# A fused attention and expert kernel whose attention order is planned anew

## The chip, the cores and the metric

The kernel runs on one core of a Trainium2 chip. The metric is the device time of one execution in microseconds (us). TensorE (PE) multiplies matrices and writes to PSUM, VectorE (DVE), ScalarE (ACT) and GpSimd (POOL) work on tiles, and SyncE's queue (SP) issues the transfers. PEld is TensorE's load of stationary operands, which overlaps its matmuls.

## What is computed

Causal attention over 2 x 12 heads of 448 positions and 64 channels, then two expert layers on the 896 x 768 result, all in fp32:

```python
scores = scale * np.matmul(q, k.transpose(0, 1, 3, 2))
scores = np.where(mask, -1000000000.0, scores)          # causal
attn = np.exp(scores - np.max(scores, axis=-1, keepdims=True))
attn = attn / (np.sum(attn, axis=-1, keepdims=True) + 1e-09)
x = np.matmul(attn, v)          # then heads side by side: 896 x 768
h = np.maximum(np.maximum(x @ w1, x @ w2), x @ w3)      # 768 -> 768
y = h @ w_out
u = y @ w_in                                            # 768 -> 2048
g = np.where(u > 0.0, u, np.exp(np.minimum(u, 0.0)) - 1.0)
out = g @ w_out2
```

The weights arrive as 64-bit words (the host's view of doubles) and are made into two fp32r parts, hi and lo, on the chip.

## The kernel before

Heads go in 12 pairs (`pair(p)`). The keys and queries of a head are cut into blocks of 128: three full ones and a last one of 64 (`R`). For a pair, in order of what needs what:

- `load` brings q and k of both heads (448 KB), `load_v` brings v (256 KB, keys padded with zeros to 512), both on SP's queue. Three buffers each.
- `scores` in three groups (`SCORES`, g = 0 for query blocks 2 and 0, g = 1 for the last block, g = 2 for block 1) into PSUM banks named `s`; there are 4 (`SBANKS`), and a pair needs 5: two heads times groups 0 and 2, and one bank for both heads' group 1.
- `least` (VectorE, L268) adds the mask, negates, stores the tile `pr` and reduces each row; it frees the score bank. `exps` (ScalarE, L278) takes the exponential and sums it into `l`.
- `guard` (GpSimd, L282) adds 1e-9 to the sums, `inverse` (VectorE, L287) takes the reciprocal, `normalise` (GpSimd, L291) multiplies the rows, seven tiles a pair.
- `turn` (five groups, `TURNS`, 16 transposes of 128 columns a pair) transposes blocks into PSUM banks named `pt`, of which there are two; `turned` (ScalarE or VectorE, L207) copies them to `th`, and the last block's 64 keys to `th_r`.
- `values` (L325) multiplies with v, four steps a pair: three over 128 keys and a last one (c = 3) over the 64 last keys. fp32 products stand as two instructions each in the trace.
- `x_hi` (ScalarE) and `x_lo` (VectorE) split the result for the expert layers.

Three blocks of the first expert layer (`AHEAD`, tile `ph`, 18 matmuls each) and the making of their weights (`weight_steps`, L142 to L159) are put among the attention's work.

The order is not written by hand. Every step is a task of the class `Plan`, with a cost per engine that it may run on, tasks that it follows, buffers that it takes and gives, and a rank. `order` repeats: for each task whose predecessors are placed it works out when it could begin and on which engine it would end first; it takes the earliest beginning; among the tasks of that engine that could begin within `SLACK` of it, it places the one of least rank. `LAG` is the planned time from an engine's end to another's start, `SWITCH` what a change of matmul kind (`mode`) adds to TensorE's start. What comes out is issued in that order, so each engine's queue and SP's queue run it as it stands. Before, rank is (pair, number of the step), `SWITCH` is 90 ns and `SLACK` 100 ns.

Behind the attention the products of the expert layers follow in program order; the conversion of their first weight (f = 1) is issued after the last `x_lo`.

Of the kernel before, what the change touches and what calls it, by code (L numbers as in the profile page):

```python
# [8 lines left out]
F32 = mybir.dt.float32  # L9
# [19 lines left out]
W_LEAST = 2.0 ** -15  # L29
W_MOST = 122876.0  # L30
AHEADS = 3
PAIRS = 3
THS = 2
SBANKS = 4


class Plan:
# [6 lines left out]


    LAG = {"PE": 210, "ACT": 150, "DVE": 125, "POOL": 90, "DMA": 2000}
    SLACK = 100
    SWITCH = 90

    def __init__(self, slots):  # L50
        self.slots = {k: [0] * n for k, n in slots.items()}
        self.parts, self.tasks, self.mode = {}, [], None

    def add(self, fn, args, engines, rank, after=(), takes=(), gives=(), mode=None):
        t = {"fn": fn, "args": args, "engines": engines, "rank": rank, "after": [a for a in after if a],
             "takes": list(takes), "gives": list(gives), "mode": mode}
        self.tasks.append(t)
        return t

    def begins(self, t, free):  # L60
        ready = {}
        for e, cost in t["engines"].items():
            at = free[e] + (self.SWITCH if e == "PE" and t["mode"] != self.mode else 0)
            for a in t["after"]:
                at = max(at, a["end"] + (0 if a["eng"] == e else self.LAG[a["eng"]]))
            for k in set(t["takes"]):
                n = t["takes"].count(k)
                if len(self.slots[k]) < n:
# [35 lines left out]
def fused_kernel(ctx: ExitStack, tc: tile.TileContext, qk, v, w1, w2, w3, wo, wi2, wo2, outT):  # L104
    nc = tc.nc
# [75 lines left out]
    with ExitStack() as s1:  # L181
# [13 lines left out]
        with ExitStack() as s2:  # L195
# [15 lines left out]
            def warm(eng, n):  # L211

                idle = ps_m.tile([128, 512], F32, tag="m", name="idle")
                for _ in range(n):
                    nc.tensor.matmul(idle, ones, ones_row, start=True, stop=True)

            plan.add(warm, (8,), {"PE": 3500}, (-1,), takes=["m"], gives=["m"])

# [3 lines left out]

            TURNS = (((0, 0, (0, 1, 2)),), ((1, 0, (0, 1, 2)),), ((0, 1, (1, 2)), (1, 1, (1, 2))),
                     ((0, 2, (2,)), (1, 2, (2,)), (None, NB, (NB,))), tuple((None, c, (NB,)) for c in range(NB)))

            def heads(i):
                return (None,) if i == NB else (1, 0)

            def pair(p):
# [97 lines left out]

# [7 lines left out]

                if p == 0:
                    cut = (slice(0, 2 * C), slice(2 * C, S))
                    got = [plan.add(load, (part,), {"DMA": 1000}, (p, 0), takes=["qk"] * (n == 0))  # L340
                           for n, part in enumerate(cut)]
                    order = (2, 0, 1)
                else:
                    got = [plan.add(load, (slice(0, S),), {"DMA": 2000}, (p, 0), takes=["qk"])]
                    order = (0, 1, 2)
                got_v = plan.add(load_v, (), {"DMA": 1000}, (p, 0.5), takes=["v"])
                done, first = {}, None
                for g in order:
                    need = got[:1] if g == 2 else got
                    ws = [min(C * (i + 1), S) for i in SCORES[g]]  # L350
                    js = heads(SCORES[g][0])
                    s = plan.add(
                        scores, (g,), {"PE": sum(120 + int(1.67 * w) for w in ws)}, (p, 1), need, takes=["s"] * len(js),
                        gives=["qk"] * (g == order[-1]), mode="s")
                    for j in js:
                        a = plan.add(
                            least, (g, j), {"DVE": sum(75 + int(1.06 * w) for w in ws)}, (p, 2), [s, first],
                            takes=["pr"] * (first is None), gives=["s"])
                        first = first or a
                        a = plan.add(exps, (g, j), {"ACT": sum(278 + int(0.84 * w) for w in ws)}, (p, 3), [a])  # L360
                        for i in SCORES[g]:
                            done[i, j] = a
                flat = {}
                for part in PARTS:
                    mine = [ij for ij, n in COLS.items() if part[0] <= n < part[1]]
                    a = plan.add(guard, part, {"POOL": 240}, (p, 4), [done[ij] for ij in mine])
                    a = plan.add(inverse, part, {"DVE": 65}, (p, 4), [a])
                    for i, j in sorted(mine, key=lambda ij: -ij[0]):
                        w = min(C * (i + 1), S)
                        flat[i, j] = plan.add(normalise, (i, j), {"POOL": 240 + int(0.84 * w)}, (p, 5), [a])  # L370
                ths, begun = [], None
                for t, blocks in enumerate(TURNS):
                    need = {(i, j) for j, c, q in blocks for i in q}
                    n = sum(len(q) for _, _, q in blocks)
                    a = plan.add(
                        turn, (t,), {"PE": 108 * n}, (p, 6), [begun] + [flat[ij] for ij in sorted(need, key=str)],
                        takes=["pt"] + ["th"] * (t == 0), gives=[("pr", p, len(TURNS))], mode="pt")
                    begun = begun or a
                    ths.append(plan.add(
                        turned, (t,), {"ACT": 55 + int(0.84 * C * n) + 60 * (t == 3),  # L380
                                       "DVE": 70 + int(1.04 * C * n) + 70 * (t == 3)},
                        (p, 7), [a], gives=["pt"]))
# [6 lines left out]
                a = plan.add(x_hi, (), {"ACT": 420}, (p, 9), [prev])  # L389
                return plan.add(x_lo, (), {"DVE": 540}, (p, 9), [a], gives=["m"])  # L390

            xs_done = [pair(p) for p in range(B * NPAIR)]

# [2 lines left out]
            def weights(k):  # L396
# [8 lines left out]
                for s, (eng, cost) in enumerate((  # L405
                        ("DMA", 4200), ("DVE", 580), ("DVE", 580), ("DVE", 580), ("DVE", 920), ("DVE", 920),
                        ("ACT", 740), ("DVE", 830))):
                    t = plan.add(
                        step, (), {eng: cost}, (GATES[k] + 1.9, s), [t or xs_done[GATES[k]]], takes={0: ["raw"], 1: ["f"]}.get(s, []),
                        gives={5: ["raw"], 7: ["f"]}.get(s, []))  # L410
                return t

            def block(k, ready):
# [14 lines left out]

                t = ready
                for c in range(NK):  # L430
                    t = plan.add(product, (c,), {"PE": 610}, (20 + k if c == 0 else 0, c), [t, ready, xs_done[c if k == 0 else NK - 1]],
                        takes=["m"] * (c == 0), mode="x")
                return plan.add(keep, (), {"DVE" if n else "ACT": 540 if n else 420}, (0, k), [t], gives=["m"])

            kept = None
            for k in range(len(AHEAD)):
# [123 lines left out]
```

## Time and profile before

| | us |
|---|---|
| median of three runs | 508.65 (508.29 to 509.17) |
| the profiled execution, its own time | 505.65 |
| its span, first to last instruction | 503.9 |
| TensorE busy in the span | 496.9 |
| VectorE, ScalarE, GpSimd busy | 364.5, 186.5, 51.9 |

In the rows below a timeline row is: start, duration, engine, line, operation, written tile <- read tiles, tile of the array (rows x columns, for TensorE), shape, count, and in brackets the idle time before it with what ended it. Consecutive instructions of one kind are merged in one row. TensorE's matmuls are pipelined and their ends are modelled, so starts are read, not ends.

### The profile page before, as it was taken

How to read it: one execution, taken by the hardware profiler on the slowest of the kernel's cores; microseconds unless marked ns; L12 is line 12 of the kernel's file. 1: busy time of each engine (PE TensorE's matmuls, PEld its weight loads, DVE VectorE, ACT ScalarE, POOL GpSimd, SP SyncE). 2: the span in 40 equal slices, each digit the busy share in tenths (PEclk: the TensorE clock that was granted, in tenths of full speed). 3: DMA queues.
4: the chain of work that ended last, by engine and by line, in shares of the span. 5: the costliest groups of instructions: out<-in, count | busy, mean ns of one | idle time of the engine just before them, and what ended most of it. 6: DMA issues, size and time to landing. Idle time of an engine off the chain costs nothing.

```text
span 503.9 us, 6971 instructions
## 1 busy us (share of the span) xinstructions
PE 496.9 (99%) x2600; PEld 426.2 (85%) x2600; DVE 364.5 (72%) x687; ACT 186.5 (37%) x432; POOL 51.9 (10%) x119
## 2 busy tenths in 40 slices
PE   8999999999999999999999999999999999999997
PEld 3556755699999999999999999999999999999996
DVE  4687966289987877787787898889878667667310
ACT  5978778422222122122214445545544111111100
POOL 3856365200000000000000000000000000000000
PEclk9999999999999999999999999999999999999999
DMA  6435720023532333233223323313332344344000
GB/s 212 154 117 170 246 84 24 1 110 141 185 129 69 120 125 123 75 117 126 88 100 126 87 101 125 123 68 124 104 88 80 118 149 144 112 152 140 1 36 36
DMA packets 13968, 55.88 MB, mean 111 GB/s; under 512 B 1520, under 2 KB 3568, under 8 KB 13936
## 3 DMA queue, kind: packets, MB, share of 16 engines
q1 hardware_dynamic: 13936, 55.45, 33.3%
q8 instruction: 20, 0.33, 0.3%
q14 instruction: 12, 0.10, 0.1%
HBM read 52.69 MB, written 2.75 MB: 110 GB/s over the span
## 4 chain that ended last, share of the span: by engine, by line
PE 93%; DVE 2%; ACT 2%; DMA 1%; POOL 1%; issue 1%; SPq 0%; POOLq 0%; ACTq 0%; DVEq 0%
PE ph L173 9%; PE ph L174 9%; PE ph L176 9%; PE pg L173 8%; PE pg L174 8%; PE pg L176 8%; PE po L176 8%; PE po L174 8%; PE po L173 8%; PE s L254 4%; PE pt L301 4%; PE o L325 3%; PE py L173 3%; PE py L176 3%; PE py L174 3%; DMA qk<-in_qk 1%
## 5 line engine op out<-in xcount | busy, mean ns | idle before, releaser
L173 PE MATMUL ph<-x,hi_w 128*128 128x448 f32 x216 | 79.3, 367 | 0.0
L174 PE MATMUL ph<-x,hi_w 128*128 128x448 f32 x216 | 78.9, 365 | 0.0
L173 PE MATMUL pg<-y,hi_wi 128*128 128x448 f32 x192 | 70.6, 367 | 0.0
L174 PE MATMUL pg<-y,hi_wi 128*128 128x448 f32 x192 | 70.6, 367 | 0.0
L173 PE MATMUL po<-g,hi_wo 128*128 128x448 f32 x192 | 70.1, 365 | 0.0
L174 PE MATMUL po<-g,hi_wo 128*128 128x448 f32 x192 | 70.1, 365 | 0.0
L159 ACT CAST hi_wo<-f_wo 128x768 fp32r<-128x768 f32 (+1 forms) x24 | 18.8, 783 | 125.3 <-PE po L174 56.4
L176 PE MATMUL ph<-x,lo_w 128*128 128x448 f32 x216 | 64.2, 365 | 0.0
L176 PE MATMUL po<-g,lo_wo 128*128 128x448 f32 x192 | 55.3, 365 | 0.0
L176 PE MATMUL pg<-y,lo_wi 128*128 128x448 f32 x192 | 55.0, 367 | 0.0
L126 DVE TENSOR_TENSOR lo_wo<-f_wo,hi_wo 128x768 fp32r<-128x768 f32 (+1 forms) x24 | 21.4, 891 | 32.1 <-ACT hi_wo L159 32.1
L173 PEld LDWEIGHTS ph<-x,hi_w 128*128 128x128 f32 x216 | 40.6, 188 | 3.3
L176 PEld LDWEIGHTS ph<-x,lo_w 128*128 128x128 f32 x216 | 40.6, 188 | 3.2
L174 PEld LDWEIGHTS ph<-x,hi_w 128*128 128x128 f32 x216 | 40.6, 188 | 3.1
L159 ACT CAST hi_w<-f_w 128x768 fp32r<-128x768 f32 x18 | 15.1, 837 | 73.3 <-PE ph L174 45.4
L173 PEld LDWEIGHTS pg<-y,hi_wi 128*128 128x128 f32 x192 | 36.0, 188 | 3.4
L176 PEld LDWEIGHTS pg<-y,lo_wi 128*128 128x128 f32 x192 | 36.0, 188 | 3.4
L174 PEld LDWEIGHTS pg<-y,hi_wi 128*128 128x128 f32 x192 | 36.0, 188 | 3.4
L174 PEld LDWEIGHTS po<-g,hi_wo 128*128 128x128 f32 x192 | 36.1, 188 | 2.9
L176 PEld LDWEIGHTS po<-g,lo_wo 128*128 128x128 f32 x192 | 36.1, 188 | 2.9
L173 PEld LDWEIGHTS po<-g,hi_wo 128*128 128x128 f32 x192 | 36.0, 188 | 2.8
L278 ACT ACTIVATE pr<-pr,nmx 128x384 f32<-128x384 f32 (+1 forms) x72 | 35.8, 502 | 5.4 <-DVE nmx L268 5.0
(76 smaller groups left out, 814.7 us busy)
## 6 DMA issues: line engine op xcount, KB each, us to landing
raw_w<-in_w SPq DMA_DIRECT2D x18, 768.0 KB, 4.4
raw_wi<-in_wi SPq DMA_DIRECT2D x16, 768.0 KB, 4.3
raw_wo<-in_wo SPq DMA_DIRECT2D x12, 768.0 KB, 4.4
raw_wo<-in_wo SPq DMA_DIRECT2D x12, 640.0 KB, 4.0
qk<-in_qk SPq DMA_DIRECT2D x11, 448.0 KB, 3.4
v<-in_v SPq DMA_DIRECT2D x12, 256.0 KB, 2.7
out_t<-ot SPq DMA_DIRECT2D x12, 224.0 KB, 3.2
qk<-in_qk SPq DMA_DIRECT2D x1, 256.0 KB, 3.3
```

The costliest lines, as they stand in the source:

```text
L126: return eng.tensor_tensor(out=out, in0=a, in1=b.bitcast(F32), op=ALU.subtract)
L159: nc.scalar.copy(hi, fb)
L173: nc.tensor.matmul(ps, hi[:, c, :], xs[cc][:, 0, :], start=(cc == 0), stop=False)
L174: nc.tensor.matmul(ps, hi[:, c, :], xs[cc][:, 1, :], start=False, stop=False)
L176: nc.tensor.matmul(ps, lo[:, c, :], xs[cc][:, 0, :], start=False, stop=(cc == total - 1))
L254: nc.tensor.matmul(out, u["qk"][own, 0, C * i:w], u["qk"][own, 1, :w], start=True, stop=True, skip_group_check=True)
L278: nc.scalar.activation(pr, pr, AF.Exp, bias=u["nmx"][:, n:n + 1], scale=-1.0, accum_out=u["l"][:, n:n + 1])
L301: nc.tensor.transpose(pt[:e - C * c, at:at + C], u["pr", j, i][:, C * c:e], ident)
L325: nc.tensor.matmul(u["o"][D * j:D * (j + 1), C * c:], u["v"][:R, j, c] if c == NB else u["v"][:, j, c], u["th_r"][:, j] if c == NB else u[ ...
```

## The change

Ranks are now pair + lead, with one lead per kind of work (table `LEADS`), ties in order of addition. `SLACK` is 80. A change of matmul kind has a charge by the two kinds. Four pairs may hold their tiles in place of three, and a pair takes its place at its first scores instead of its first `least`. `guard` and `normalise` may run on VectorE or GpSimd, whichever would end first in the plan. The last keys' tile `th_r` has 128 rows; two such tiles are set to zero once by GpSimd, only the first 64 rows are written later, and the product reads all 128 rows of both operands. Some planned costs are altered (loads, scores, values, warming), which changes the plan and no instruction.

```diff
-PAIRS = 3
+PAIRS = 4
+LEADS = {
+    "exps": 12.19, "guard": 2.16, "inverse": 4.13, "keep": -4.94, "least": 4, "load": -9.21, "load_v": -4.69,
+    "normalise": 5.1, "product": 17.18, "scores0": -0.81, "scores1": 1.15, "scores2": 0.27, "step": -5.89,
+    "turn0": -10.05, "turn1": 0.24, "turn2": 1.83, "turn3": 1.96, "turn4": 1.17, "turned0": -7.64, "turned1": 8.07,
+    "turned2": 12.56, "turned3": -1.06, "turned4": 10.91, "values0": 2.99, "values1": 2.02, "values2": -11.03,
+    "values3": -0.06, "warm": -14.64, "x_hi": 3, "x_lo": -5.37,
+}
-    SLACK = 100
-    SWITCH = 90
+    SLACK = 80
+    SWITCH = {("s", "pt"): 150, ("pt", "s"): 95, ("pt", "x"): 0, ("x", "pt"): 0, ("o", "pt"): 60}
+    SWITCHES = 100
...
+    def switch(self, mode):
+        return 0 if mode == self.mode else self.SWITCH.get((self.mode, mode), self.SWITCHES)
...
-            at = free[e] + (self.SWITCH if e == "PE" and t["mode"] != self.mode else 0)
+            at = free[e] + (self.switch(t["mode"]) if e == "PE" else 0)
...
-            plan.add(warm, (8,), {"PE": 3500}, (-1,), takes=["m"], gives=["m"])
+            plan.add(warm, (8,), {"PE": 4200}, 0, takes=["m"], gives=["m"])
...
+            th_r = [thp.tile([C, 2, R], F32, name=f"th_r{n}", bufs=1) for n in range(THS)]
+            for t in th_r:
+                nc.gpsimd.memset(t, 0.0)
...
-                        u["th_r"] = thp.tile([R, 2, R], F32, tag="th_r", name=f"th_r{p}")
+                        u["th_r"] = th_r[p % THS]
...
-                            copy(eng, u["th_r"], pt[:R, 2 * w:2 * w + C].rearrange("k (j q) -> k j q", j=2))
+                            copy(eng, u["th_r"][:R], pt[:R, 2 * w:2 * w + C].rearrange("k (j q) -> k j q", j=2))
...
-                            u["o"][D * j:D * (j + 1), C * c:], u["v"][:R, j, c] if c == NB else u["v"][:, j, c],
+                            u["o"][D * j:D * (j + 1), C * c:], u["v"][:, j, c],
...
-                        scores, (g,), {"PE": sum(120 + int(1.67 * w) for w in ws)}, (p, 1), need, takes=["s"] * len(js),
-                        gives=["qk"] * (g == order[-1]), mode="s")
+                        scores, (g,), {"PE": (960, 870, 540)[g]}, p, [*need, begun],
+                        takes=["s"] * len(js) + ["pr"] * (begun is None), gives=["qk"] * (g == order[-1]), mode="s")
...
-                    a = plan.add(guard, part, {"POOL": 240}, (p, 4), [done[ij] for ij in mine])
+                    a = plan.add(guard, part, {"POOL": 240, "DVE": 65}, p, [done[ij] for ij in mine])
...
-                        flat[i, j] = plan.add(normalise, (i, j), {"POOL": 240 + int(0.84 * w)}, (p, 5), [a])
+                        flat[i, j] = plan.add(
+                            normalise, (i, j), {"POOL": 240 + int(0.84 * w), "DVE": 60 + int(0.62 * w)}, p, [a])
...
-                        values, (c,), {"PE": 120 + int(1.67 * (S - C * c))}, (p, 8),
-                        [ths[t] for t in need] + [got_v, prev], takes=["m"] * (c == 0),
-                        gives=["th", "v"] * (c == NB), mode="o" if c < NB else "r")
+                        values, (c,), {"PE": (805, 540, 380, 130)[c]}, p, [ths[t] for t in need] + [got_v, prev],
+                        takes=["m"] * (c == 0), gives=["th", "v"] * (c == NB), mode="o")
```

The expert blocks' first products rank at k + 17.18 and their other products at -20 + 17.18; the weights' steps at the pair of their gate - 5.89. The other ranks follow the table.

## Rows read from the trace of the kernel before

**Rows 1.** The page, busy us, share of the span, instructions.

```profile
PE 496.9 (99%) x2600; PEld 426.2 (85%) x2600; DVE 364.5 (72%) x687; ACT 186.5 (37%) x432; POOL 51.9 (10%) x119
```

**Rows 2.** Stretches: length, busy us by engine, granted clock, DMA share, GB/s.

```profile
0.00:100.97 100.97, 97.51 (x638) 57.90 (x638) 64.35 (x240) 75.41 (x239) 51.88 (x119) 1.00 0.39 126
100.97:500.50 399.53, 399.42 (x1966) 368.32 (x1962) 300.15 (x447) 110.58 (x193) 0.00 (x0) 1.00 0.32 107
```

**Rows 3.** TensorE's timeline, the first scores.

```profile
4.26 3.12 PE L254 MATMUL s<-qk 64*128 64x256 f32 x16
8.44 4.84 PE L254 MATMUL s<-qk 64*128 64x384 f32 x28 [1.06 <-DMA qk<-in_qk]
```

**Rows 4.** SP's issues near 2 us; their transfers, us to landing last.

```profile
2.07 0.59 SPq L242 DMA_DIRECT2D v<-in_v  x1
...
2.70 0.43 SPq L238 DMA_DIRECT2D qk<-in_qk  x1
...
v<-in_v SPq DMA_DIRECT2D x1, 256.0 KB, 5.1
...
qk<-in_qk SPq DMA_DIRECT2D x1, 448.0 KB, 5.6
```

**Rows 5.** TensorE's timeline, one period in the middle of the attention.

```profile
64.68 1.84 PE L325 MATMUL o<-th,v 128*64 128x448 f32 x12
66.45 0.33 PE L325 MATMUL o<-th_r,v 64*64 64x64 f32 x4
66.71 0.87 PE L301 MATMUL pt<-ident,pr 128*128 128x128 f32 x6
67.51 0.70 PE L254 MATMUL s<-qk 64*128 64x256 f32 x4
68.14 0.88 PE L301 MATMUL pt<-ident,pr 128*128 128x128 f32 x6
68.86 0.27 PE L301 MATMUL pt<-ident,pr_None 128*64 128x128 f32 x1
69.06 1.14 PE L254 MATMUL s<-qk 64*128 64x384 f32 x8
70.13 0.55 PE L301 MATMUL pt<-ident,pr_None 128*128 128x128 f32 x3
70.60 0.97 PE L254 MATMUL s<-qk 64*64 64x448 f32 x4
71.50 1.84 PE L325 MATMUL o<-th,v 128*64 128x448 f32 x12
```

**Rows 6.** The same timeline, two groups of scores in a row.

```profile
56.72 1.57 PE L254 MATMUL s<-qk 64*128 64x256 f32 x12
58.21 0.47 PE L173 MATMUL ph<-x,hi_w 128*128 128x448 f32 x1
```

**Rows 7.** Stretches again: the next period, columns as in rows 2.

```profile
71.50:78.32 6.82, 6.82 (x50) 3.81 (x48) 4.27 (x22) 5.89 (x20) 3.85 (x10) 1.00 0.16 41
```

**Rows 8.** The same timeline, first and last of four waits within the attention.

```profile
35.78 0.44 PE L301 MATMUL pt<-ident,pr 128*128 128x128 f32 x2 [0.25 <-ACT th L207]
...
98.94 1.84 PE L325 MATMUL o<-th,v 128*64 128x448 f32 x12 [0.57 <-ACT th L207]
```

**Rows 9.** GpSimd's and VectorE's timelines: four normalisings, weight steps, together and apart.

```profile
28.82 3.28 POOL L291 TENSOR_SCALAR pr<-pr,r 128x384 f32<-128x384 f32 x4 [0.38 <-DVE r L287]
...
73.92 1.85 POOL L291 TENSOR_SCALAR pr<-pr,r 128x384 f32<-128x384 f32 x4 [0.38 <-DVE r L287]
...
29.14 0.83 DVE L144 TENSOR_SCALAR f_w<-f_w 128x768 f32<-128x768 f32 x1
...
113.34 0.56 DVE L144 TENSOR_SCALAR f_w<-f_w 128x768 f32<-128x768 f32 x1
```

**Rows 10.** Timelines of VectorE and TensorE where the next weight is first read.

```profile
109.55 1.81 DVE L126 TENSOR_TENSOR lo_w<-f_w,hi_w 128x768 fp32r<-128x768 f32 x2
...
112.01 0.36 PE L173 MATMUL ph<-x,hi_w 128*128 128x448 f32 x1
```

More of the change, by code (lines that the diff above doesn't have):

```diff
@@ L52, in __init__, with add @@
         self.parts, self.tasks, self.mode = {}, [], None
-    def add(self, fn, args, engines, rank, after=(), takes=(), gives=(), mode=None):
-        t = {"fn": fn, "args": args, "engines": engines, "rank": rank, "after": [a for a in after if a],
-             "takes": list(takes), "gives": list(gives), "mode": mode}
+    def add(self, fn, args, engines, pair, after=(), takes=(), gives=(), mode=None):
+        lead = LEADS.get(f"{fn.__name__}{args[0]}" if args else None, LEADS.get(fn.__name__))
+        t = {"fn": fn, "args": args, "engines": engines, "pair": pair, "rank": (pair + lead, len(self.tasks)),
+             "after": [a for a in after if a], "takes": list(takes), "gives": list(gives), "mode": mode}
         self.tasks.append(t)
         return t
+    def switch(self, mode):
+        return 0 if mode == self.mode else self.SWITCH.get((self.mode, mode), self.SWITCHES)
     def begins(self, t, free):
@@ L339, in pair @@
                     cut = (slice(0, 2 * C), slice(2 * C, S))
-                    got = [plan.add(load, (part,), {"DMA": 1000}, (p, 0), takes=["qk"] * (n == 0))
+                    got = [plan.add(load, (part,), {"DMA": 1000 if n else 2200}, p, takes=["qk"] * (n == 0))
                            for n, part in enumerate(cut)]
@@ L343, in pair @@
                 else:
-                    got = [plan.add(load, (slice(0, S),), {"DMA": 2000}, (p, 0), takes=["qk"])]
+                    got = [plan.add(load, (slice(0, S),), {"DMA": 2000}, p, takes=["qk"])]
                     order = (0, 1, 2)
-                got_v = plan.add(load_v, (), {"DMA": 1000}, (p, 0.5), takes=["v"])
-                done, first = {}, None
+                got_v = plan.add(load_v, (), {"DMA": 1200}, p, takes=["v"])
+                done, begun = {}, None
                 for g in order:
@@ L352, in pair @@
                     s = plan.add(
-                        scores, (g,), {"PE": sum(120 + int(1.67 * w) for w in ws)}, (p, 1), need, takes=["s"] * len(js),
-                        gives=["qk"] * (g == order[-1]), mode="s")
+                        scores, (g,), {"PE": (960, 870, 540)[g]}, p, [*need, begun],
+                        takes=["s"] * len(js) + ["pr"] * (begun is None), gives=["qk"] * (g == order[-1]), mode="s")
+                    begun = begun or s
                     for j in js:
[L356 to L360, printed above, removed]
+                        a = plan.add(least, (g, j), {"DVE": sum(75 + int(1.06 * w) for w in ws)}, p, [s], gives=["s"])
+                        a = plan.add(exps, (g, j), {"ACT": sum(278 + int(0.84 * w) for w in ws)}, p, [a])
                         for i in SCORES[g]:
@@ L365, in pair @@
                     mine = [ij for ij, n in COLS.items() if part[0] <= n < part[1]]
-                    a = plan.add(guard, part, {"POOL": 240}, (p, 4), [done[ij] for ij in mine])
-                    a = plan.add(inverse, part, {"DVE": 65}, (p, 4), [a])
+                    a = plan.add(guard, part, {"POOL": 240, "DVE": 65}, p, [done[ij] for ij in mine])
+                    a = plan.add(inverse, part, {"DVE": 65}, p, [a])
                     for i, j in sorted(mine, key=lambda ij: -ij[0]):
                         w = min(C * (i + 1), S)
-                        flat[i, j] = plan.add(normalise, (i, j), {"POOL": 240 + int(0.84 * w)}, (p, 5), [a])
+                        flat[i, j] = plan.add(
+                            normalise, (i, j), {"POOL": 240 + int(0.84 * w), "DVE": 60 + int(0.62 * w)}, p, [a])
                 ths, begun = [], None
@@ L375, in pair @@
                     a = plan.add(
-                        turn, (t,), {"PE": 108 * n}, (p, 6), [begun] + [flat[ij] for ij in sorted(need, key=str)],
+                        turn, (t,), {"PE": 109 * n}, p, [begun] + [flat[ij] for ij in sorted(need, key=str)],
                         takes=["pt"] + ["th"] * (t == 0), gives=[("pr", p, len(TURNS))], mode="pt")
@@ L380, in pair @@
                         turned, (t,), {"ACT": 55 + int(0.84 * C * n) + 60 * (t == 3),
-                                       "DVE": 70 + int(1.04 * C * n) + 70 * (t == 3)},
-                        (p, 7), [a], gives=["pt"]))
+                                       "DVE": 70 + int(1.04 * C * n) + 70 * (t == 3)}, p, [a], gives=["pt"]))
                 prev = None
@@ L385, in pair @@
                     prev = plan.add(
-                        values, (c,), {"PE": 120 + int(1.67 * (S - C * c))}, (p, 8),
-                        [ths[t] for t in need] + [got_v, prev], takes=["m"] * (c == 0),
-                        gives=["th", "v"] * (c == NB), mode="o" if c < NB else "r")
-                a = plan.add(x_hi, (), {"ACT": 420}, (p, 9), [prev])
-                return plan.add(x_lo, (), {"DVE": 540}, (p, 9), [a], gives=["m"])
+                        values, (c,), {"PE": (805, 540, 380, 130)[c]}, p, [ths[t] for t in need] + [got_v, prev],
+                        takes=["m"] * (c == 0), gives=["th", "v"] * (c == NB), mode="o")
+                a = plan.add(x_hi, (), {"ACT": 420}, p, [prev])
+                return plan.add(x_lo, (), {"DVE": 540}, p, [a], gives=["m"])
             xs_done = [pair(p) for p in range(B * NPAIR)]
@@ L408, in weights @@
                     t = plan.add(
-                        step, (), {eng: cost}, (GATES[k] + 1.9, s), [t or xs_done[GATES[k]]], takes={0: ["raw"], 1: ["f"]}.get(s, []),
+                        step, (), {eng: cost}, GATES[k], [t or xs_done[GATES[k]]], takes={0: ["raw"], 1: ["f"]}.get(s, []),
                         gives={5: ["raw"], 7: ["f"]}.get(s, []))
@@ L430, in block @@
                 for c in range(NK):
-                    t = plan.add(product, (c,), {"PE": 610}, (20 + k if c == 0 else 0, c), [t, ready, xs_done[c if k == 0 else NK - 1]],
+                    t = plan.add(product, (c,), {"PE": 610}, k if c == 0 else -20, [t, ready, xs_done[c if k == 0 else NK - 1]],
                         takes=["m"] * (c == 0), mode="x")
-                return plan.add(keep, (), {"DVE" if n else "ACT": 540 if n else 420}, (0, k), [t], gives=["m"])
+                return plan.add(keep, (), {"DVE" if n else "ACT": 540 if n else 420}, 0, [t], gives=["m"])
             kept = None
```

## The prediction

> **What bounds the kernel now.** I read the page's busy shares first: TensorE is busy 99% of the span [rows 1], so only time on TensorE's queue counts. The stretches come next. Up to 100.97 us stand the attention and three early expert blocks; from there to 500.50 us TensorE is busy 399.42 of 399.53 us [rows 2], at the full granted clock (1.00, the 2.4 GHz level). The change leaves all work behind the attention as it is, so it can move the time only by ending the attention earlier, and whatever is won there passes to the end one for one, as long as the first weight tile of the next part still comes in time (below). TensorE's order of time then shows what those 100.97 us are made of. The first scores start at 4.26 us and the next ones wait 1.06 us for a load [rows 3]. From there TensorE is nearly without a gap: four waits, 1.27 us in all, of which the first and the longest stand in [rows 8]. One pair's period in the middle of the stage is 6.82 us (64.68 to 71.50) and holds no wait at all [rows 5], while ScalarE is busy 5.89 us of it, VectorE 4.27 and GpSimd 3.85 [rows 7]. So the stage is bound by TensorE, and what is left in a period is what TensorE pays when it goes from one kind of matmul to another.
>
> That price can be read from the starts in [rows 5]. Six, seven and three transposes take 0.80, 0.92 and 0.47 us to the next kind: 0.11 us each and 0.14 us for the visit. Scores of 256, 512 and 448 columns take 0.63, 1.07 and 0.90 us; two such groups in a row (768 columns) take 58.21 - 56.72 = 1.49 us [rows 6] against 0.63 + 1.07 = 1.70 apart, so a visit to the scores costs 0.21 us. A period has three visits to the transposes, three to the scores, one to the values. The last-keys products (four instructions, 64x64) take 66.71 - 66.45 = 0.26 us.
>
> **The change, part by part.** The sum is made against the profiled execution (505.65 us, span 503.9); the median of the three runs without a profile is 508.65, 3.0 us longer, and I carry the difference over to it.
>
> (a) First loads. Ranks of equal start decide among loads, and the new leads put every load of q and k (-9.21) ahead of every load of v (-4.69). So the first seven issues on SP become q/k of pair 0 (two), q/k of pairs 1 and 2, then the three of v. Now v of pair 0 goes ahead of pair 1's q and k: issued at 2.07 and 2.70 us, landed 5.1 and 5.6 us later, at 7.2 and 8.3 [rows 4]. The 448 KB between those landings took 1.1 us, so taking 256 KB out of the way brings pair 1's load forward by 256/448 x 1.1 = 0.6 us, 0.7 with the earlier issue. The wait is 1.06 us, the gain lies between 0.6 and 1.06; I take 0.7, the lower row, because the bytes ahead set it. The v that is moved back then lands at some 7.6 + 1.1 + 0.6 = 9.3 us by the same rate; TensorE is at scores until 13.2 us [rows 3], so nobody reads it before. The new charge of 4200 for the warming matmuls alters planned times alone; they are the same eight matmuls.
>
> (b) Last keys over zero rows. The four 64x64 instructions become 128x64 ones, as the twelve before them are. By columns at the rate of those twelve (1.77 us for 448 + 320 + 192 = 960 columns [rows 5], 1.84 ns a column) 64 columns are 0.12 us against 0.26. No row shows a 128x64 fp32 product of 64 columns, so it is bounded: 0 saved if 0.26 is a floor for four short instructions, 0.14 if columns rule. I take 0.13, near the upper end, because a transpose, also short, runs at 0.11 a piece with nothing added inside its visit. Twelve pairs: 1.6 us (0 to 1.7). The two added memsets of 128 columns fall on GpSimd's queue before its first guard, where it idles for microseconds; the copy into the 64 used rows is unchanged.
>
> The row says only that four small matmuls cost as much as 140 columns. The Trainium skill, "TensorEngine Tiling", section Key Properties, says that a change of tiling mode, unlike a change of tile, drains TensorE; by it the 0.26 holds a drain from 128x64 to 64x64 that (b) removes. The same page's section Instruction Overhead puts some 60 cycles on every matmul however short, by which part of the 0.26 would stay. By the first the sum is as I give it, by the second alone it is up to 1.6 us less.
>
> (c) Fewer changes of kind. Before, a change costs 90 ns in the plan and SLACK is 100, so a change of kind never put a task out of reach and rank alone chose. After, a change to or from the scores is charged 95 to 150 and SLACK is 80: a task of the kind that TensorE is in wins wherever one is ready. How far this goes is bounded by banks: two hold transposes, so after two turns the third waits for a copy, and five turns a pair make at least 2.5 visits in place of 3. Four hold scores, of which a pair needs five: 1.25 visits at least. At the least, nothing is saved; at the most (3 - 2.5) x 0.14 + (3 - 1.25) x 0.21 = 0.44 us a pair, 4.8 us over eleven periods. ScalarE's 5.89 us a period, still 0.9 us below TensorE's, does not stop this. I take 0.18 a pair, half a visit of each kind (0.07 + 0.105), 2.0 us: the leads also rank kinds, and a bank that is freed too late breaks a run of one kind.
>
> (d) Four pairs held, and normalising on VectorE too. They give the plan more ready work where TensorE waits: the four gaps (1.27 us [rows 8]). The two longest lie at the end, where only the last pair is left and nothing but an expert block could fill them. I take 0.4 us (0 to 1.27).
>
> (e) What VectorE's new work costs. It gets some of the seven normalisings and guards a pair, against them GpSimd is lightened. On its own a 768-wide tensor_scalar takes it 0.56 us, so a 384-wide one about 0.3 by halves (an estimate). But the trace shows the two engines hindering one another: four normalisings that take GpSimd 1.85 us take 3.28 when VectorE runs two tensor_scalars beside them, and those take 0.83 instead of 0.56 [rows 9]. Behind such an instruction on VectorE are queued the reductions that free score banks, and TensorE waits for those; GpSimd's late tiles hold the next transposes. The plan has no term for this. Nothing lost at the least, since both engines have over 2.5 us of idle time a period; at the most each pair loses 0.6 us (below). I take 0.6 us in all.
>
> Sum: 0.7 + 1.6 + 2.0 + 0.4 - 0.6 = 4.1 us less, 501.5 for the profiled execution, **504.5 us** for the median.
>
> Cover behind the attention: the conversion of the next weight starts at the last pair's x, its two low parts end at 111.36 us, and TensorE reads the first at 112.01 [rows 10]: 0.65 us of slack at least. It moves with the attention's end, so I cost it at nothing; if the last x came over 0.65 us later after the last values than now, the rest would be a TensorE gap.
>
> **The rivals.**
> First, the collision of VectorE and GpSimd sets the pace (slower). Its place is each pair's normalising; its price is what [rows 9] show, 3.28 - 1.85 = 1.43 us on GpSimd for four tiles, of which TensorE sees what goes beyond the turn's slack. It outweighs the gain from 4.7/11 = 0.43 us of TensorE wait a pair; at 0.55 a pair the time is 508.65 - 4.7 + 6.1 = 510.0. For it: a static order with thinner slack, and a plan without this term. Against: after today's collision at 29 to 32 us TensorE's first wait is 0.25 us, at 35.78 [rows 8], and it names a copy.
>
> The Trainium skill, "SBUF — State Buffer", section Who interferes with whom, states that GpSimd and a VectorE tensor_scalar in a two-port mode exclude each other for a whole instruction. The trace agrees in that both were lengthened, and by that rule this rival is the mechanism to fear.
>
> Second, the order does not regroup: banks break every run, three visits of each kind stay, and the 0.26 is a floor. Only (a) is left, with (d) and (e) cancelling: 508.65 - 0.7 = 507.95. For it: the leads move ranks in all directions (values of block 2 first, its copies last), which has no visible reason.
>
> Third, grouping goes to its bound: 0.7 + 1.6 + 4.0 + 0.8 = 7.1 less, 501.5. For it: the rule of SLACK below the charge. Against: copies on ScalarE at 5.89 of 6.82 us would have to come exactly in time.
>
> **How the numbers follow.** Forecast 57%, collision 14%, no regrouping 14%, full grouping 15%. A measurement of this kernel tells about 0.2%, 1.0 us, from no change. Faster by more than that (below 507.6): 57 + 15 = 72%. Same: 14%. Slower: 14%. The range reaches to 501.0 on one side, just past the third rival, and to 509.2 on the other; outside it are most of the first rival and a little below the third, about 18%.
>
> **What would show it.** (a) The wait for q and k at 8.44 us falls below 0.4 us. (b) Four 128x64 instructions of 64 columns from start to next start in 0.12 to 0.14 us. (c) Fewer than three visits to the transposes and the scores in a pair, a period near 6.5 us. (e) VectorE instructions on line L291's successor, some of them far over 0.35 us beside GpSimd, and TensorE waits that name them. The attention's last values end near 97 us in place of 100.97. Wrong it would be if TensorE's waits in the stage grow beyond 3 us, or if the period stays at 6.8.

## The result and the profile after

The changed kernel takes 502.46 us (median of four executions, 502.04 to 503.07) against 508.47 for the kernel before beside it: ratio 0.988, 95% interval 0.9863 to 0.9898, 6.0 us less. The profiled executions, though, lie only 505.65 - 502.18 = 3.5 us apart. That gap between the two comparisons is half of what there is to explain.

The changed kernel's page and its stretches (columns as in [rows 1] and [rows 2]; the first stretch now ends where the last values do):

```profile
PE 494.2 (99%) x2600; PEld 427.0 (85%) x2600; DVE 375.9 (75%) x727; ACT 186.6 (37%) x433; POOL 34.7 (7%) x80
```

```profile
0.00:97.47 97.47, 94.79 (x638) 58.66 (x638) 75.69 (x280) 75.46 (x240) 34.66 (x80) 1.00 0.40 130
97.47:497.00 399.53, 399.44 (x1966) 368.31 (x1962) 300.21 (x447) 110.57 (x193) 0.00 (x0) 1.00 0.32 107
```

Against [rows 2] the attention is 3.5 us shorter (97.47 for 100.97) and the part behind it as long as before (399.53). VectorE has 11 us more work there, GpSimd 17 less. TensorE's waits in this stretch (waited for: us in all, times, longest us):

```profile
PE pt L321 <- POOL pr L311: 0.5, 2, 0.3
PE pt L321 <- DVE pr L311: 0.5, 2, 0.3
PE s L274 <- DVE nmx L288: 0.4, 1, 0.4
PE s L274 <- DMA qk<-in_qk: 0.3, 1, 0.3
```

The wait for pair 1's q and k, 1.06 us in [rows 3], is 0.3 here; the two waits at the stage's end ([rows 8]) are gone, and four new ones name the tiles that are now shared between VectorE and GpSimd. TensorE's timeline shows what became of the regular period of [rows 5]:

```profile
7.41 4.04 PE L274 MATMUL s<-qk 64*128 64x384 f32 x24 [0.31 <-DMA qk<-in_qk]
...
38.06 4.75 PE L274 MATMUL s<-qk 64*128 64x384 f32 x28
42.74 0.55 PE L321 MATMUL pt<-ident,pr_None 128*128 128x128 f32 x3
43.12 0.60 PE L321 MATMUL pt<-ident,pr 128*128 128x128 f32 x4
43.66 1.84 PE L345 MATMUL o<-th,v 128*64 128x448 f32 x12
45.32 0.28 PE L345 MATMUL o<-th_r,v 128*64 128x64 f32 x4
45.54 0.44 PE L321 MATMUL pt<-ident,pr 128*128 128x128 f32 x2
...
91.84 0.97 PE L345 MATMUL o<-th,v 128*64 128x448 f32 x4
92.75 0.55 PE L321 MATMUL pt<-ident,pr 128*128 128x128 f32 x3
93.13 0.49 PE L321 MATMUL pt<-ident,pr_None 128*128 128x128 f32 x3
93.55 1.08 PE L345 MATMUL o<-th,v 128*64 128x320 f32 x8
```

There is no period any more. At 38.06 us TensorE runs scores for 4.7 us without a break, nearly two pairs' worth; at the end it goes to and fro between the values of one pair and the transposes of the next, and the values of a pair stand in pieces. All 16 instructions of a pair's values take 45.54 - 43.66 = 1.88 us where they took 2.03.

For the whole stage I add up, over TensorE's matmuls from the first scores to the last values, the time from each start to the next, by kind (a wait counts to the instruction ahead of it), and count the visits:

| kind | us before | us after | visits before | visits after |
|---|---|---|---|---|
| scores | 33.13 | 30.43 | 28 | 12 |
| transposes | 27.94 | 27.56 | 32 | 31 |
| values | 24.34 | 23.53 | 12 | 17 |
| expert products | 11.30 | 11.69 | 4 | 7 |
| sum | 96.71 | 93.21 | 76 | 67 |

The largest fall is at the scores, 2.7 us. Of this 1.03 us lie at the start: pair 1's scores begin at 7.41 us in place of 8.44 [rows 3], 0.75 us of it by the shorter wait and the rest within pair 0's scores, where it was not looked into. The values' 0.8 us is what zero rows save less what five more visits cost. Over all kinds there are nine changes of kind fewer, 67 visits for 76.

### The profile page after: what moved, and what is told of

Read it like the earlier page. It is cut to its first block, busy times and chain, and to the rows that moved or that the text cites. A ratio compares the mean times of both kernels' runs of the same rounds, so it can differ in the third digit from the quotient of the medians.

```text
span 500.4 us, 6931 instructions
## 1 busy us (share of the span) xinstructions
PE 494.2 (99%) x2600; PEld 427.0 (85%) x2600; DVE 375.9 (75%) x727; ACT 186.6 (37%) x433; POOL 34.7 (7%) x80
## 4 chain that ended last, share of the span: by engine, by line
PE 92%; DVE 3%; ACT 1%; DMA 1%; POOL 1%; issue 0%; SPq 0%; ACTq 0%; POOLq 0%
PE ph L188 9%; PE ph L189 9%; PE ph L191 9%; PE pg L191 8%; PE pg L189 8%; PE pg L188 8%; PE po L191 8%; PE po L189 8%; PE po L188 8%; PE s L274 4%; PE pt L321 3%; PE o L345 3%; PE py L188 3%; PE py L191 3%; PE py L189 3%; DMA qk<-in_qk 1%
```

## Experiments

Each kernel of this section is either the kernel before or the changed one with one thing altered. "End" is the start of the first product behind the last values, read from the profile; medians are those of the executions.

**The kernel before, unchanged.** No edit.

> The kernel before, unchanged. The timed runs of the two kernels lie 6.0 us apart (508.47 and 502.46), the two traces only 3.5 us (505.65 and 502.18). Theory one: the trace of before is a fast execution of the same program, and a typical one has a stall of some 2.8 us that the change also removed; then this profile takes about 508.5 us and shows the stall in one place, most likely in the attention or where the next weight is first read (0.65 us of slack there). Theory two: that execution was on a chip or in a state that is 0.55% faster throughout; then this profile takes 508.5 us, too, but every stretch is 0.5% longer and no wait has grown. If it takes 505.7 again, profiled executions are shorter than others.

Measured: 509.06 us (508.35 to 509.39), ratio to its own kind 1.0002 (0.9993 to 1.001); the profiled execution took 509.29 us with a span of 507.5, 3.6 us more than the trace on which the prediction rests. Its first long scores and its second stretch:

```profile
8.92 4.84 PE L254 MATMUL s<-qk 64*128 64x384 f32 x28 [2.13 <-DMA qk<-in_qk]
```

```profile
101.38:504.00 402.62, 402.62 (x1966) 368.28 (x1962) 300.07 (x447) 110.52 (x192) 0.00 (x0) 1.00 0.31 107
```

The load's wait is 1.07 us longer, of which 0.4 is left at the attention's end (101.38). The other 3.2 us lie behind the attention, where the same 1,966 matmuls take 402.6 us in place of 399.5. Neither theory holds: there is no stall, and not every stretch is longer. From start to start the first 810 products behind the attention run at 206.7 ns each, those of the earlier trace at 202.7; the 576 of the next layer (tile `pg`) run at 205.3 and the last 576 at 202.7 in both. The granted clock is 1.00 in both. Between 120 and 240 us, in this kernel and in the changed one:

```profile
120.00:240.00 120.00, 120.00 (x583) 108.99 (x582) 94.10 (x136) 25.16 (x40) 0.00 (x0) 1.00 0.33 118
```

```profile
120.00:240.00 120.00, 120.00 (x594) 111.20 (x593) 95.95 (x139) 24.31 (x39) 0.00 (x0) 1.00 0.33 116
```

So one program has two paces, 3.2 us apart. In the comparison of this run all 35 executions of the kernel before took 507.9 to 509.9 us. In the two later ones both paces stand side by side: of 37 executions 12 took 505.3 to 506.1 us and 25 took 508.3 to 510.8. All eight of the changed kernel took 502.0 to 503.1.

**Short matmuls between the weight tiles**, in the kernel before:

```diff
+        cut_l, cut_r = (nc.const_aps.tensor(1.0, [128, w], BF16) for w in (128, 64))
+
+        def cut():
+            idle = psum("cut")
+            nc.tensor.matmul(idle[:, :64], cut_l, cut_r, start=True, stop=True)
...
                         hi, lo = load_w(w[f], NK, f"w{n}_{f}")
+                    if n == 0:
+                        cut()
...
             hi, lo = load_w(wo[f], NK, f"wo_{f}")
+            cut()
```

> The kernel before with one short matmul of another type (64 columns, read by nobody) ahead of each of the eleven weight tiles f = 1 to 5 of the first expert layer and f = 0 to 5 of its output layer. In the runs so far the 800 products of these two layers went either all at 202.7 ns or all at 206.7 ns, in one program even (before: 505.3 to 505.8 us in three of 13 executions, 508.4 to 510.8 in ten). Theory one: the pace is a rhythm into which loads and matmuls fall at the entry of a row of products and which then holds; with eleven new entries it is drawn anew at each, so tiles of both paces stand in one trace. Theory two: the pace belongs to the whole execution (clock, chip, place of the tiles in memory); then all tiles have one pace in spite of the cuts. The cuts cost some 0.2 us each, 2 us in all.

Measured: ten executions between 506.71 and 507.46 us, none apart from the others, while the kernel before beside them split again (nine from 505.43 to 506.07, fifteen from 508.28). The eleven cuts cost some 0.14 us each (400.57 us for the part against 399.05). In the trace eleven of the twelve rows of products run at 202.6 to 202.8 ns a step, one at 206.6. That one and the next, each from its cut on:

```profile
229.70 0.20 PE L450 MATMUL cut<-const-bfloat16-1.0 128*128 128x64 bf16 x1
229.74 0.46 PE L173 MATMUL py<-h,hi_wo 128*128 128x448 f32 x1
230.03 0.36 PE L174 MATMUL py<-h,hi_wo 128*128 128x448 f32 x1
...
231.89 0.37 PE L176 MATMUL py<-h,lo_wo 128*128 128x448 f32 x1
...
237.26 0.20 PE L450 MATMUL cut<-const-bfloat16-1.0 128*128 128x64 bf16 x1
237.30 0.45 PE L173 MATMUL py<-h,hi_wo 128*128 128x448 f32 x1
237.59 0.36 PE L174 MATMUL py<-h,hi_wo 128*128 128x448 f32 x1
...
239.40 0.36 PE L176 MATMUL py<-h,lo_wo 128*128 128x448 f32 x1
```

From 230.03 to 231.89 us there are nine steps of 207 ns, from 237.59 to 239.40 nine of 201 (202.8 over the whole row). Theory one holds: the pace changes from one entry to the next, and within a row it stays. The second falls by this trace, which has both paces in one execution, and the executions no longer split. The changed kernel shows it without cuts: its early expert block at 62.09 us runs at 206.6 ns, the one at 69.26 us at 202.6. From here on the attention's end is compared, which the pace hardly touches.

**The changed kernel, unchanged.** No edit.

> The changed kernel, unchanged. It shows the spread: the attention's end at 97.5 us give or take the first loads' landing (0.5 us), and whether the products behind it fall into the fast rhythm (202.7 ns, some 502.5 us) in all executions, as in the four so far, or also into the slow one (some 505.7 us).

Measured: 502.43 us (502.3 to 502.9), end at 97.77, products at 202.7 ns.

**First loads in the new order alone**, in the kernel before; every engine's order stays:

```diff
-                for fn, eng, args in plan.order():
+                steps = plan.order()
+                first = [t for t in steps if t[0].__name__ == "load"][:4]
+                for fn, eng, args in first + [t for t in steps if t not in first]:
```

> The kernel before with only the first transfers in another order: q and k of pairs 0 to 2 ahead of v of pairs 0 to 2; all engines' orders are those of before. Theory one: the wait for pair 1's q and k falls from 1.06 to about 0.3 us and the rest follows, 0.7 to 1.0 us less. Rival: the start is bound by score banks and VectorE's reductions soon after, and the gain is lost in waits before 20 us: 0 to 0.3 us less.

Measured: 508.38 us against 508.93, ratio 0.9987 (0.9978 to 0.9996), 0.55 us less; the end at 100.68. The wait for q and k was still 1.69 us in the profiled execution, beside 2.13 in the unchanged kernel of the same comparison. Its start of pair 1's scores, 8.21 us, lies within what the old order of loads gives by itself (8.11 to 8.92 in the four traces of the kernel before, its zero rows and its cuts), so the landing's spread is as large as the gain; the gain is read from the medians.

**Last keys over zero rows alone**, in the kernel before: two zeroed tiles of 128 rows for `th_r`, all 128 rows read, plan and order of before.

> The kernel before with the last keys over zero rows alone; TensorE's order is that of before. Theory one (columns rule, and the change of tile was the cost): the values of a pair take 1.88 us from first start to the next kind instead of 2.03, as in the changed kernel, so 12 x 0.15 = 1.8 us less than before. Rival (four short products have a floor): 0 to 0.3 us less.

Measured: 507.76 us, ratio 0.998 (0.997 to 0.999), 1.2 us less; end at 99.59. One pair's values, to be laid beside [rows 5]:

```profile
64.19 1.84 PE L329 MATMUL o<-th,v 128*64 128x448 f32 x12
65.85 0.28 PE L329 MATMUL o<-th_r,v 128*64 128x64 f32 x4
66.07 0.66 PE L305 MATMUL pt<-ident,pr 128*128 128x128 f32 x4
```

1.88 us in place of 2.03, and 24.34 - 22.57 = 1.77 us over all values; 0.46 came back as waits at the transposes (27.91 to 28.37). Of the 0.15 us a pair, 0.10 is won before the last four instructions: the last of the twelve takes 0.16 us to the next start in place of 0.26, as both now have the same tile of the array. The four themselves fell from 0.26 to 0.22. From start to start they take 6, 50, 6 and 153 ns, before 7, 100, 6 and 149: the first two now take 0.06 us, which is what their columns give, and the 0.15 at the end is the step to the transposes, as long as before.

**The same taken out of the changed kernel**: operands cut to 64 rows.

```diff
-                            u["o"][D * j:D * (j + 1), C * c:], u["v"][:, j, c],
-                            u["th_r"][:, j] if c == NB else u["th"][:, c, j, C * c:], start=(c == 0), stop=(c == NB),
+                            u["o"][D * j:D * (j + 1), C * c:], u["v"][:R, j, c] if c == NB else u["v"][:, j, c],
+                            u["th_r"][:R, j] if c == NB else u["th"][:, c, j, C * c:], start=(c == 0), stop=(c == NB),
```

> The changed kernel, but the last keys' product reads 64 rows of both operands again, so it runs as 64x64; plan and order are those of the changed kernel. Theory one (the change of tile costs 0.15 us a pair wherever it stands): the attention ends 12 x 0.15 = 1.8 us later than the changed kernel's 97.47 us, near 99.3. Rival (in this order the cost hides): 97.5 to 98. In the part behind the attention the first 800 matmuls run at 202.7 or at 206.7 ns each, which the run shows beside it: 3.2 us that are no part of this question.

Measured: end at 98.44, 503.27 us. The values cost 1.47 us more (25.00 against 23.53); 0.5 us of it is won back at the transposes (27.04 against 27.56), whose tiles have had more time.

**The new charges alone**, in the kernel before: `SLACK` 80 and the table of `SWITCH`, ranks, three pairs and engines of before.

> The kernel before with only the charges per change of kind and SLACK 80: ranks are those of before. TensorE's order has 20 visits to the scores in place of 28 and 28 to the transposes in place of 32. Theory one (a visit to the scores costs 0.21 us and one to the transposes 0.14, and the plan's order holds on the chip): 8 x 0.21 + 4 x 0.14 = 2.2 us less than before. Rival (leads and the fourth pair are needed; with three pairs the runs of one kind meet tiles that are not ready): new waits eat it, 0 to 0.8 us less or slower.

Measured: 514.8 us, ratio 1.0121 (1.0106 to 1.0136), 5.9 us more; in the profiled execution, the longest of four (516.52), the end is at 111.86, 10.5 us later than in the unchanged kernel's. The times lie less far apart than the ends because the products of this trace ran at the quick pace. TensorE's waits:

```profile
PE pt L305 <- POOL pr L295: 2.3, 2, 1.2
PE o L329 <- ACT th L211: 2.2, 5, 0.6
PE pt L305 <- ACT th L211: 1.5, 4, 0.5
PE s L258 <- DVE nmx L272: 1.4, 2, 1.0
PE s L258 <- DMA qk<-in_qk: 1.3, 2, 1.1
```

Ten visits fewer (66 against 76 in the traces, the scores eight fewer) and much slower: TensorE stays at one kind and then stands before tiles of the next that are not ready, 7.4 us in the first four of these lines.

**Ranks of before in the changed kernel**: pair and number of the step in place of pair and lead, all else as changed.

> The changed kernel planned with the ranks of before (pair, then number of the step) and the new charges, four pairs, VectorE and the zero rows. TensorE's order has 19 visits to the scores, 27 to the transposes and 12 to the values against 12, 31 and 17: in all fewer. Theory one (visits alone count): 7 x 0.21 - 4 x 0.14 - 5 x 0.15 = 0.2 us from the changed kernel, attention's end near 97.6. Rival (the leads keep tiles ready: before with the new charges alone and ranks by step lost 10.5 us in the attention to waits): waits of several us on transposes, attention's end at 100 us or later.

Measured: 513.78 us, ratio 1.01 (1.0085 to 1.0115); end at 106.51, 9.0 us later than the changed kernel's, with 6.6 us of waits within the stage apart from the first load's:

```profile
PE pt L334 <- DVE pr L324: 1.9, 3, 1.1
PE o L358 <- ACT th L235: 1.8, 3, 0.7
...
PE pt L334 <- ACT th L235: 1.1, 3, 0.4
PE pt L334 <- ACT th_r L235: 1.1, 2, 0.9
...
PE pt L334 <- POOL pr L324: 0.7, 1, 0.7
```

The rival holds: this order has fewer visits than the changed kernel's (64 against 67) and loses to it by far. The four pairs and VectorE's help do not mend it; the leads do.

**Old charges in the changed kernel**: `SLACK` 100, one charge of 90 ns, leads and all else as changed.

> The changed kernel planned with SLACK 100 and one charge of 90 ns; leads, four pairs, VectorE and the zero rows stay. TensorE's order has 23 visits to the scores, 36 to the transposes and 18 to the values, against 12, 31 and 17. Theory one (visits are what the charges save): 11 x 0.21 + 5 x 0.14 + 0.15 = 3.2 us more than the changed kernel, attention's end near 100.6. Rival (leads and depth of four pairs do the work): within 1 us of 97.47.

Measured: 508.57 us, ratio 1.000 (0.997 to 1.003), with five of ten executions at either pace (506.5 to 507.1 and 510.0 to 510.5); end at 102.57, 5.1 us later, 1.1 of them at the first load (a wait of 1.4 us for 0.3). The scores cost 1.6 us more (that wait among it), the transposes 2.6, the expert products 1.0. The leads without the charges are no better than the kernel before (its ends: 100.97 and 101.38); the two parts of the plan are worth something only together.

**Three pairs in the changed kernel**: `PAIRS = 3`.

> The changed kernel planned with three pairs held in place of four, all else as changed. TensorE's order has 16 visits to the scores, 33 to the transposes and 18 to the values against 12, 31 and 17. Theory one (the fourth pair is what lets the scores stand in long rows): 4 x 0.21 + 2 x 0.14 + 0.15 = 1.3 us by visits, and more by waits for tiles, attention's end at 99 us or later against 97.47. Rival (three pairs are enough for these leads): within 0.5 us of 97.47.

Measured: end at 99.92, 2.4 us later; a median of 507.83 us with three executions of ten at 504.5 to 504.7, since its products fall into either pace. It has six visits more than the changed kernel (73 against 67). One wait of 1.0 us stands at the expert products for an `x_lo`, 0.5 us more than in the changed kernel at the first load.

**GpSimd alone, VectorE alone, in the changed kernel's order** (the first kernel's edit; the second has `"DVE"`):

```diff
                 for fn, eng, args in plan.order():
+                    if fn.__name__ in ("guard", "normalise"):
+                        eng = "POOL"
```

> The changed kernel with the same order of everything, but each guard and each normalising on GpSimd in place of VectorE. Theory one (VectorE's help shortens the way from exponential to transposes, and the order was planned for it): the transposes wait for GpSimd's tiles, more than 0.5 us of such waits, and the attention ends 1 to 4 us later than 97.47. Rival (the collision of the two engines costs as much as the help gives): it ends within 0.5 us of 97.47 or earlier.

> The changed kernel with the same order of everything, but every guard and normalising on VectorE; GpSimd is left with the constants. The mirror of the run in which GpSimd did them all and the attention ended 3.1 us later. Theory one (VectorE is the engine with little to spare: 75.7 us busy of 96.5, and GpSimd's 34.7 us would come to it as some 18): reductions come late, TensorE waits for score banks and transposes, attention's end 1 to 5 us later than 97.47. Rival (the collision of the two engines is what is left to win): with no GpSimd instruction beside it VectorE's normalisings take 0.3 us for 384 columns in place of 0.50, and the end is at 97.5 or earlier.

Measured: with GpSimd alone (505.39 us) the end is at 100.54, 3.1 us later, and TensorE waits 4.3 us in five places for its tiles; with VectorE alone it is at 103.62, 6.1 us later (508.6 us):

```profile
PE pt L321 <- DVE pr L311: 3.8, 5, 1.1
PE s L274 <- DVE nmx L288: 1.8, 3, 0.7
...
PE o L345 <- DVE th L222: 0.5, 1, 0.5
PE pt L321 <- DVE th L222: 0.5, 1, 0.5
```

The first line is VectorE's own lateness with the tiles, the second the score banks that its reductions free late, the last two its copies.

Both rivals fall: the order needs both engines. An order planned for one of them was not built. VectorE's normalisings by shape (count, busy us, mean ns of one), first beside GpSimd in the changed kernel, then alone:

```profile
L311 DVE TENSOR_SCALAR pr<-pr,r 128x384 f32<-128x384 f32 x10 | 4.6, 496 | 0.1
L311 DVE TENSOR_SCALAR pr<-pr,r 128x256 f32<-128x256 f32 x9 | 4.2, 471 | 0.0
```

```profile
L311 DVE TENSOR_SCALAR pr<-pr,r 128x384 f32<-128x384 f32 x24 | 9.5, 415 | 0.1
L311 DVE TENSOR_SCALAR pr<-pr,r 128x256 f32<-128x256 f32 x24 | 7.4, 345 | 0.0
```

Alone they take 415 and 345 ns, beside GpSimd 496 and 471.

## Why the prediction was right, and where not

The time (502.46) lies in the range and on the side that was forecast, 2.0 us below the 504.5 named. Two steps were off, in opposite directions: the carry-over and the sum for the attention.

**The carry-over from profile to median** is the step that failed. I took the 3.0 us between the profiled execution and the median as a constant of the measurement. It was the pace of 810 products: the trace of before is one of the executions at 202.7 ns, the median one at 206.7. The changed kernel's profile and median (502.18 and 502.46) differ by 0.3. So I predicted 501.5 for the profile, 0.7 too low, and then added 3.0 where 0.3 was due: 2.7 - 0.7 = 2.0. The sentence that the change "can move the time only by ending the attention earlier" fell with it; what was won in the attention did pass to the end, 3.5 us between the two traces of equal pace. Of the 6.0 us some 3 are the attention's (between executions of equal pace: 505.3 to 506.1 against 502.0 to 503.1), and some 3 come from the changed kernel's products having fallen into the quick pace in all eight executions. No step of the prediction had these 3 us. At the slower pace the changed kernel would have taken some 505.7 us (502.46 + 3.2, an estimate), in the range as well.

**The sum for the attention** was 4.1 us and the traces show 3.5. That it came so near is in part luck, as its terms came about otherwise than forecast. Read from the traces, (a) gave 1.0 us, (b) 0.8 to 1.5 (at the end, or at the values alone), and 1.0 to 1.7 are left for (c) to (e), which were to give 1.8.

**(a)** 0.7 forecast; 0.55 alone (0.9987), 1.03 between the two traces. The mechanism is right; the size can't be told better than that, as the landing moves by 0.8 us between executions of one order. One reading was wrong: in the changed kernel the loads of v stand behind a fourth pair's q and k as well and are issued from 7.52 us; no wait of TensorE names them.

**(b)** 1.6 forecast; TensorE saved 1.77 us, of which 1.2 reached the end alone and 0.8 in the changed kernel. Size right on the engine, too large at the end, as waits took some of it. The 0.26 was not where most of the cost lay: 0.10 of the 0.15 us a pair is won ahead of the four, at the change of tile. That is what the Trainium skill, "TensorEngine Tiling", section Key Properties, says of a drain at a change of tiling mode, and the trace agrees with it at this place. It does not at every one: a transpose in a 128x64 tile among those in 128x128 tiles takes 0.11 us from start to start like the others. The sign of 0.12 to 0.14 us for the four did not come (0.22), because the reading from start to next start holds the step to the transposes, 0.15 us before and after; no floor for short products shows, since the first two of the four take the 0.06 us of their columns.

**(c)** 2.0 forecast, by half a visit less of each kind. The order did something else: scores fell from 28 visits to 12, transposes only from 32 to 31, values rose from 12 to 17 and expert products from 4 to 7. The bound of 1.25 visits a pair was wrong: VectorE frees score banks while TensorE is at the scores, so one visit can run through 28 instructions with four banks. The kernel before already had such a visit in [rows 3]. During the one at 38.06 us VectorE reads one score bank after another:

```profile
39.24 0.56 DVE L288 CUSTOM_DVE_ANT_0 pr<-s,mask 128x384 f32<-128x384 f32 x1 [0.15 <-PE s L274]
...
41.96 0.56 DVE L288 CUSTOM_DVE_ANT_0 pr<-s,mask 128x384 f32<-128x384 f32 x1 [0.16 <-PE s L274]
```

At 0.21 us, 16 visits would be 3.4 us; apart from the start the scores fell by 1.7, and 0.66 went back to the values and 0.4 to the products. The price belongs to the change of kind and not to the scores alone: from start to start a transpose takes 0.11 us within its visit, 0.165 as the first after scores or values and 0.20 as the last before them, some 0.15 a change. By that price the nine changes fewer are some 1.3 us (an estimate from these steps), in place of the 2.0 forecast. And the reason was only half of it. I had the charges as the cause; alone they made the kernel 1.2% slower, and with four pairs and both engines but the old ranks still 1.0%. The leads, whose odd values I had counted against the plan, decide whether the tiles are ready when TensorE stays. The altered planned costs and the place that a pair now takes at its first scores were not run by themselves.

**(d) and (e)** 0.4 won and 0.6 lost forecast. The two waits at the end are gone; 1.0 us of waits now names normalised tiles and 0.4 a score bank, so the loss was under-sized, and the price of one normalising (0.3 us by halves) too: 0.415 alone. In all, the waits apart from the load's went from 1.27 to 1.5 us, as the two terms together had it. But without VectorE's help the same order is 3.1 us slower: the help was worth more than I gave it.

**The rivals.** The collision came, in one place at a price as read: at 59.58 us two normalisings of 256 columns take GpSimd 2.27 us (two such at 65.71 us take 0.93), while VectorE works on a weight, and TensorE waits 0.34 and 0.20 us for them.

```profile
59.58 2.27 POOL L311 TENSOR_SCALAR pr<-pr,r 128x256 f32<-128x256 f32 x2 [1.62 <-DVE r L307]
...
60.75 0.76 DVE L157 TENSOR_SCALAR f_w<-raw_w 128x768 int32<-128x768 int32 x1
61.54 0.71 DVE L159 TENSOR_SCALAR f_w<-f_w 128x768 f32<-128x768 f32 x1
```

It did not come in every pair, as the rival needed. No regrouping and grouping to the bound were both wrong by kind: the scores went past the bound, the transposes did not move.

The cover behind the attention held: it moved along with the end.

## What to carry to other kernels

Fewer changes of kind on TensorE are worth some 0.15 us each, and only where the tiles for a longer stay are ready: the charges without matching priorities made the attention 10 us longer than before, and the priorities without the charges left it 5 us longer than both together. Where products of 64 rows stand behind products of 128 rows, zero rows that keep the array's tile unchanged save the change (0.15 us a pair here, of which two thirds reached the end when this was done alone). Before a difference between a trace and a median is carried over, look for it in the trace of a second execution: here it was as large as the gain.

## What the hardware showed that was not expected

A long row of fp32r products of 448 columns, a weight load for each, has two steady paces at the same granted clock (1.00): 202.7 and 206.7 ns from start to start. A row keeps its pace over hundreds of matmuls; the same program falls into either from one execution to the next, and both occur within one execution. In these two layers the pace changes only at an entry: with a short matmul of another type ahead of each weight tile eleven rows of twelve were quick and no execution was slow as a whole. What TensorE did before the row matters too: the three kernels that issue its work in the changed kernel's order (`a_64_rows`, `a_pool_same_order`, `a_dve_same_order`) were quick in all 18 executions, as the changed one was in its eight, while `a_pairs3` and `a_old_charges` split. What at the entry decides stays open (the first two gaps differ by a few ns: 310 and 199 ns in the changed kernel's quick row, 314 and 200 in the slow row of the kernel before), and so does why this order was quick each time; a cut at the head of the changed kernel's products wasn't tried. In the next layer, where every trace shows 205.3 ns, the cause wasn't looked for.
